# A planned attention kernel: other planned ACT durations in the front, fewer groups in an output phase, output weights split one round after their loads

## The chip, the cores and the metric

The kernel runs on one core of one Trainium2 chip. The time is the device time in microseconds (us) of one execution; the median of three runs is compared. The core has five engines with a queue each: TensorE (PE in the profile, its weight loads PEld), VectorE (DVE), ScalarE (ACT), GpSimd (POOL) and SyncE (SP), which issues transfers. They meet only through semaphores, and each works through its queue in order.

## The reference

A gate mixes two attention branches over the same input x of 2048 positions and 512 features, all in float32.

```python
g = sigmoid((x * gate_w).sum(-1, keepdims=True))
a = A_ref(x, A_wqkv, A_wo)   # 32 heads of 16; each position sees 8 positions, 2 apart, behind it
b = B_ref(x, B_wq, B_wk, B_wv, B_wo)   # 32 query heads of 16, one key and value head, all 2048 positions
return g * a + (1 - g) * b
```

Branch A is a local, dilated attention: softmax over 8 logits for each position and head. Branch B is full attention, where `softmax(q @ k.T / 4)` has 32 x 2048 x 2048 entries. Each branch ends with a product with a 512 x 512 matrix of output weights.

## The kernel before, in words

**Units and steps.** Branch B is cut into 32 units (4 blocks of 512 queries by 8 groups of 4 heads) and each unit into 16 steps of 128 keys. A step computes scores of four heads (two calls of `exp_pair`, L521, each two half matmuls that use 64 rows of the array and run side by side, then one exponential of 1024 columns on ACT, L528) and adds weighted values (`weighted`, L533, eight matmuls of 32 columns at L536) into the bank `po`. There are 512 steps.

**Maxima.** The exponential needs a shift for each query that is near its largest score. So the scores are also computed once ahead of the steps, only for their maxima: 2048 half matmuls in all, of one head pair, 128 queries and 512 keys each. They are made in three forms:
- a *pair* (`fill_pair`, L375): two half matmuls into the bank `pm`, one reduction of 1024 columns on VectorE (L380);
- a *single* (`fill_one`, L384): one half matmul into `ps` or `po`, one reduction of 512 columns (L391);
- a *group* (`fill_diff`, L447, and `fill_sum`, L466): for two blocks of keys, a matmul with half their difference, whose absolute value ACT writes to SBUF (L458), and a matmul with half their sum, which VectorE adds to it and reduces (L471). A group stands for two half maxima. It moves half of the evacuation from VectorE to ACT.

The maxima of a unit must be complete, turned and stored (`filled`, `shift_a` to `shift_d`) before its first step.

**The front.** Before the steps come the projections: keys, then 14 outputs of queries ("q", L1080), then 64 outputs of branch A ("a", four quarters `gg` of 16 blocks of positions, L1081). An output is 12 pairs of half matmuls in one of the banks `pe0` and `pe1`. `stream` (L742) issues them and places singles or groups between them, so that a half of a group runs beside a half of an output. When an output of branch A is done, `a_post` (L244) copies it out with ACT (L258, L259; in the first quarter also L262).

**The planner.** The order of all instructions is fixed while the program is written, by clocks of its own: `clk["pe"]`, `clk["act"]`, `clk["dve"]`, and `pool`. `after(engine, ready, duration)` (L99) moves such a clock. The durations are constants in the code. A group is placed only if `diff_ready` (L440) holds, which among others asks that ACT's clock is at most 0.7 us ahead of TensorE's. If the next maxima are for a group and it isn't ready, the slot passes without a maximum. In the front and in an output phase, slots for groups are the only ones once the keys' sums and differences are formed.

**The steps' maxima.** In each step `fill_ready` (L902) places a pair, and a single if `singles` (L896) says that those that are left need it; a single is not placed in a unit's first step. `pause` (L912) makes maxima between steps when a unit would start without.

**Output phases.** Three times four rows of blocks of output are computed between steps (`out_phase`, L780): for each row transposes, copies and splits on ACT (`prepare` L686, `turn` L695, `out_store` L728), 24 slots of half matmuls, and groups between them through the same `stream`. The last four rows are spread over the last steps (`spread`, L825): the condition for its start stands in the loop of steps (L1184).

**GpSimd's work.** `work` (L992) is a generator of pieces for branch A's local attention on GpSimd, in 16 rounds of two; `run_pool` (L1059) issues pieces as far as 2.5 us ahead of TensorE's clock. From the start of the steps on, a round also takes entries of the list `wos` (L986): `wo_load` (L676) loads 128 rows of output weights through SP into one of two buffers, and `wo_split` (L680) splits them into a high part (ACT, L94) and a rest (GpSimd, L95).

Of the kernel before, what the change touches and what calls it, by code (L numbers as in the profile page):

```python
# [19 lines left out]
C = D // P  # L20
# [4 lines left out]
NU = NQB * NHG  # L25
# [13 lines left out]
NF = 2 * NU * 2 * 4 * 4  # L39
FMAX = 3.4028234e38  # L40
NH = NJ // 2
LEAD, M2S, M1S, PER_ROW = 3.0, 0.5, 0.3, 20


T_R, T_LAT, T_EXP, T_RED2, T_RED1, T_W, T_TTR = 0.23, 0.20, 0.92, 1.14, 0.61, 1.21, 0.66
# [3 lines left out]
def gated_mix_kernel(ctx, tc, xt, wa, wk, wq, wo_a, wo_b, out):  # L49
# [40 lines left out]
    free = {"m2": 0.0, "m1": 0.0, "e0": 0.0, "e1": 0.0, "po": 0.0, "d0": 0.0, "d1": 0.0}  # L90
# [6 lines left out]
    clk = {"pe": 0.0, "act": 0.0, "dve": 0.0}  # L97

    def after(eng, ready, dur):  # L99
        clk[eng] = max(clk[eng], ready) + dur  # L100
        return clk[eng]
# [142 lines left out]
    def a_post(gg, j, x):  # L244

        nonlocal pool
        (bank, key), n = front[x], GN + (0 if gg else VN)
        settle("add", 1)
        if j % 2 == 0:
            settle("store", 1)  # L250
            stage["t"] = p1.tile([P, GC, 2, AN], F32, name="stage", bufs=2)
        st = stage["t"]
        if gg == 0 and j < 3:
            two = wp.tile([P, GN + VN], F32, name="two", tag="aext", bufs=2)
        else:
            two = (p2 if j % 3 else pm)[0].tile([P, GN + VN], F32, name="two", tag=("two", "raw", "own")[j % 3], bufs=1)
        own = st[:, :, j % 2, :]
        nc.scalar.activation(own, bank[:, 0, :GN].rearrange("p (g n) -> p g n", g=GC), AF.Copy)  # L258
        nc.scalar.activation(two[:, :n], bank[:, 1, :n], AF.Copy)  # L259
        if gg == 0:  # L260
            vg = p1.tile([P, VN], F32, name="vg", bufs=2)
            nc.scalar.activation(vg, bank[:, 0, GN:GN + VN], AF.Copy)  # L262
        at = after("act", clk["pe"] + T_LAT, 0.8 if gg else 1.0)
        free[key] = at + 0.1

        def rest():
            nonlocal pool
            nc.gpsimd.tensor_add(own, own, two[:, :GN].rearrange("p (g n) -> p g n", g=GC))
            if gg == 0:
                nc.gpsimd.tensor_add(vst[:, j, 0:DH], vg[:, 0:DH], two[:, GN:GN + DH])  # L270
                nc.gpsimd.tensor_add(gate[:, 1, j:j + 1], vg[:, DH:DH + 1], two[:, GN + DH:GN + DH + 1])
            pool = max(pool, 1e3 * at) + (1000 if gg else 1450)
            if j % 2 == 1:
                dst = ad[gg * GC:(gg + 1) * GC, HALO:, :].rearrange("g (p j) n -> p g (j n)", j=NJ)
                tasks.append((pool / 1e3 + 0.5, lambda: nc.sync.dma_start(dst[:, :, (j - 1) * AN:(j + 1) * AN], st.rearrange("p g j n -> p g (j n)")), (), "store"))
            if j == NJ - 1:
                tasks.append((pool / 1e3 + 1.0, whole, (gg,)))

        tasks.append((at, rest, (), "add"))
# [58 lines left out]
    half = []  # L338
    tasks, shifted, pm = [], set(), []
    hooks, pool, done = [], 0.0, set()  # L340
# [20 lines left out]
    def to_go():  # L361
        return 2 * len(slots) + len(half)
# [33 lines left out]
    sel, dd, pend, group, formed, ended, wants = [], [], [], [], set(), set(), []  # L396
# [43 lines left out]
    def diff_ready():  # L440
        if not group and (ended or half or not hv or not paired()):
            return False
        odd = group[0][4] if group else 0
        now = clk["pe"]
        return len(pend) < len(dd) + 1 and free[f"d{odd}"] <= now + 0.1 and dd[0][1][odd] <= now + 0.9 and clk["act"] <= now + 0.7 and clk["dve"] <= now + 1.8

    def fill_diff():  # L447
        if not group:
            v, pr, t, kc = slots.pop(0)
            slots.pop(0)  # L450
            group.extend([(v, pr, t, kc, 0), (v, pr, t, kc, 1)])
        v, pr, t, kc, odd = group.pop(0)
        dst, until = dd[0]
        if odd:
            dd.append(dd.pop(0))
        half_mm(hv[odd], v, pr, t, kc, 1, odd)
        at = clk["pe"] + T_R + T_LAT
        nc.scalar.activation(dst[:, odd], hv[odd], AF.Abs)  # L458
        at = after("act", max(at, until[odd]), 0.52) + 0.1
        free[f"d{odd}"] = at  # L460
        pend.append((v, pr, t, kc, odd, at, dst, until))

# [56 lines left out]
    pe, pexp, exped = [], {}, {}  # L519
# [22 lines left out]
    obp, shaped = {}, set()  # L542
# [39 lines left out]
    def a_load(g, hf):  # L582
        e = wp.tile([P, HALO + NH, AN], F32, name="aext", bufs=2)
        src = ad[g]
# [3 lines left out]
    def a_scores(g, hf):  # L588
        e = aext[g]
        lg = alog[g] = p2[0].tile([P, W, NH, AG], F32, name="lg", bufs=2)  # L590
        q = e[:, HALO:HALO + NH, 0:AC]
        for w4 in range(0, W, 4):
# [67 lines left out]
    p2b = []  # L660
# [231 lines left out]
    later_rows, spread_at = [], [0.0]  # L892
# [92 lines left out]

    wos = []  # L986
    kcs = [(k, c) for k in range(2) for c in range(C)]
    for i in range(2 * C + 1):
        wos.append([(wo_load, kcs[i])] if i < 2 * C else [])
        wos[-1] += [(wo_split, kcs[i - 1])] if i else []  # L990

    def work():  # L992

        def sub(g, hf):
            yield lambda: ("max", g, hf) in done
            a_sub(g)
            hooks.append((pool + 3000, a_exp, g, ("exp", g, hf)))
            yield 500
            summing.append((g, hf))

        def sums():

            if summing and ("exp",) + summing[0] in done:
                g, hf = summing.pop(0)
                a_add_up(g)
                hooks.append((pool + 800, a_sum, g, ("sum", g, hf)))
                yield 800

        def values(g, hf):
            while ("sum", g, hf) not in done:  # L1010
                if summing:
                    yield lambda: ("exp",) + summing[0] in done
                    yield from sums()
                else:
                    yield lambda: ("sum", g, hf) in done
            yield lambda: g < 8 or p2b
            yield from a_values(g, hf)
            if g == NAG - 1:
                done.add(hf)

        def load(i):
            if i < len(order):
                yield lambda: order[i][0] // GC < ready_gg
                a_load(*order[i])
                yield 600 if i else 6200

        order = [(g, hf) for hf in range(2) for g in range(NAG)]
        extra, summing = list(wos), []
        yield from load(0)
        yield from load(1)  # L1030
        for i in range(0, len(order), 2):
            yield from a_scores(*order[i])
            hooks.append((pool + 3500, a_max, order[i][0], ("max",) + order[i]))
            for k, x in enumerate(a_scores(*order[i + 1])):
                yield x
                if k == 6:
                    yield from sub(*order[i])
                if k == 11:
                    yield from sums()
            hooks.append((pool + 3500, a_max, order[i + 1][0], ("max",) + order[i + 1]))  # L1040
            for k, x in enumerate(values(*order[i])):
                yield x
                if k == 6:
                    yield from sub(*order[i + 1])
                if k == 11:
                    yield from sums()
            yield from load(i + 2)
            yield from values(*order[i + 1])
            yield from load(i + 3)
            for _ in range(2):  # L1050
                if p2b and extra:
                    for f, a in extra.pop(0):
                        f(*a)
                    yield 1300
        assert not extra

    pieces, blocked = [work()], []
# [25 lines left out]
    last = len(lumps) - 1  # L1083
# [76 lines left out]
    for s in range(NS + 1):  # L1160
# [21 lines left out]
        k, n = outs // 4, C - (outs >= NJ - 4)  # L1182
        one = singles(s)
        if outs == NJ - 4:  # L1184
            if NU - 3 in shaped and not half and not one and not later_rows and "last" not in done:
                later_rows.append(spread(list(range(outs, NJ)), n))
            if short > 0 and steps < 2:
                pause(short)
        elif due or outs < NJ and s and kt == 0 and outs // NH in done and NHG * (k + 1) - 1 in shaped and (lead < LEAD or s >= 16 * (NHG * (k + 2) + 1)):
            if not due:  # L1190
                prepare(outs, n)
                due.append(n)
            else:
                out_phase(list(range(outs, outs + 4)), due.pop(), kt == 1)
                outs += 4
                order = (0, "m1", 2)
        elif short > 0 and steps < 2:
            pause(short)
# [83 lines left out]
```

## Time and profile before

| | us |
|---|---|
| median of 3 runs (lowest to highest) | 1512.37 (1512.18 to 1513.42) |
| the profiled execution | 1513.46 |
| its span, first to last instruction | 1511.7 |
| PE, ACT, DVE, POOL busy in it | 1479.3, 1360.6, 1117.5, 1004.4 |

The steps begin at about 319 us; before that is the front. The three output phases stand at about 881 to 917, 1047 to 1084 and 1215 to 1254 us. In the profile a row of a group of instructions names line, engine, operation, the tiles it writes and reads, and how often it stands; behind the bar come busy time, the mean of one in ns, and how long the engine was idle just before them, with what ended that. A busy PE is not a PE at its peak, since matmuls overlap.

### The profile page before, as it was taken

The numbers are of one execution on the slowest core, as the hardware profiler recorded it, in microseconds if no ns is written. First come the engines' busy times: TensorE is split into PE (matmuls) and PEld (weight loads), VectorE is DVE, ScalarE is ACT, GpSimd is POOL, SyncE is SP. The second block draws the span as 40 slices with busy tenths as digits, with TensorE's granted clock in tenths as the row PEclk, the third lists the DMA queues.
The fourth block names the chain that finished last, engine by engine and source line by source line (L and its number), as shares of the span: only waits on it lengthen the run. The fifth ranks groups of instructions, "written<-read, shape, count | busy, mean of one in ns | idle before, by whom it ended". The sixth has DMA issues, their size and how long they took to land.

```text
span 1511.7 us, 29757 instructions
## 1 busy us (share of the span) xinstructions
PE 1479.3 (98%) x10920; PEld 711.6 (47%) x10920; DVE 1117.5 (74%) x1848; ACT 1360.6 (90%) x1802; POOL 1004.4 (66%) x1770
## 2 busy tenths in 40 slices
PE   7999999989999999999999999999999999999998
PEld 4787787843333333333333354334533364333343
DVE  6668788867787787777878877877688887877401
ACT  4789999978999999999999989999899998999975
POOL 6764888877988888888788898888888330000110
PEclk9999999999999999999999999999999999999999
DMA  6542424230212112112112112220211001100000
GB/s 218 148 118 88 136 75 141 67 126 12 94 41 75 59 58 80 41 52 84 52 48 80 41 54 66 69 74 29 91 49 54 13 15 47 33 2 12 12 1 29
DMA packets 48034, 97.60 MB, mean 65 GB/s; under 512 B 10784, under 2 KB 27168, under 8 KB 43792
## 3 DMA queue, kind: packets, MB, share of 16 engines
q1 hardware_dynamic: 41216, 55.99, 12.6%
q0 software_dynamic: 5664, 37.87, 7.5%
q8 instruction: 86, 1.41, 0.4%
q10 hardware_dynamic: 1008, 1.84, 0.3%
q14 instruction: 60, 0.49, 0.1%
HBM read 69.90 MB, written 25.78 MB: 63 GB/s over the span
## 4 chain that ended last, share of the span: by engine, by line
PE 73%; ACT 3%; issue 1%; DVE 1%; DVEq 0%; ACTq 0%; DMA 0%
PE po L536 32%; PE pe L526 23%; PE pm L359 7%; PE pe L792 4%; PE ps L359 3%; ACT pexp L528 2%; PE pd L438 1%; PE ps L438 1%; PE ps L861 1%; PE pm L861 1%; PE po L438 1%; PE pe L699 0%; PE pe L1246 0%; DVE mx L380 0%; ACT woh L94 0%
## 5 line engine op out<-in xcount | busy, mean ns | idle before, releaser
L528 ACT ACTIVATE pexp<-pe 128x1024 f32<-128x1024 f32 x1021 | 982.6, 1023 | 70.1 <-PE pe L526 66.7
L380 DVE TENSOR_REDUCE mx<-pm 128x2 f32<-128x1024 f32 x474 | 579.0, 1221 | 212.2 <-PE pm L359 208.2
L536 PE MATMUL po<-pexp,vst 128*32 128x512 f32 x4096 | 546.8, 606 | 1.2 <-DVE mx L471 0.7
L526 PE MATMUL pe<-qst,kst 64*128 64x512 f32 x2042 | 498.8, 460 | 10.2 <-ACT pexp L528 10.0
L526 PEld LDWEIGHTS pe<-qst,kst 64*128 64x128 f32 x2042 | 197.5, 184 | 509.7 <-ACT pexp L528 497.4
L359 PE MATMUL pm<-kst,qst 62*128 62x512 f32 x951 | 192.2, 399 | 1.9 <-DVE mx L380 1.4
L458 ACT ACTIVATE dd<-pd 128x512 f32<-128x512 f32 x300 | 169.8, 602 | 16.0 <-PE pd L438 4.6
L596 POOL TENSOR_TENSOR pr<-aext 128x256 f32<-128x256 f32 x256 | 182.7, 742 | 0.2
L391 DVE TENSOR_REDUCE mx<-ps 128x1 f32<-128x512 f32 x257 | 174.7, 680 | 4.2 <-PE ps L359 2.1
L656 POOL TENSOR_TENSOR oa<-oa,av 128x256 f32<-128x256 f32 x224 | 164.2, 733 | 15.3
L438 PE MATMUL pd<-kcd,qst 62*128 62x512 f32 x416 | 151.2, 413 | 4.4 <-ACT dd L458 3.9
L536 PEld LDWEIGHTS po<-pexp,vst 128*32 128x32 f32 x4096 | 80.6, 108 | 146.1 <-issue 134.3
L653 POOL TENSOR_TENSOR av<-aext,lg 128x256 f32<-128x256 f32 x224 | 139.7, 624 | 12.1
L1111 PE MATMUL pe<-wah,xl 64*128 64x384 f32 (+1 forms) x504 | 133.9, 348 | 0.0
L1111 PE MATMUL pe<-wah,xh 64*128 64x384 f32 (+1 forms) x504 | 132.3, 345 | 0.3 <-ACT two L220 0.3
L1111 PE MATMUL pe<-wal,xh 64*128 64x384 f32 (+1 forms) x504 | 131.7, 346 | 0.0
L471 DVE CUSTOM_DVE_ANT_0 dd<-ps,dd 128x512 f32<-128x512 f32 x150 | 103.6, 690 | 33.6 <-PE ps L438 13.7
L471 DVE CUSTOM_DVE_ANT_0 dd<-po,dd 128x512 f32<-128x512 f32 x150 | 103.4, 690 | 20.4 <-ACT dd L458 8.0
L359 PE MATMUL ps<-kst,qst 62*128 62x512 f32 x257 | 104.3, 406 | 0.3 <-DVE mx L391 0.3
L562 POOL TENSOR_TENSOR rl<-rl,gate_t 128x16 f32<-128x16 f32 x31 | 6.9, 223 | 143.6 <-DVE rl L556 143.5
L359 PEld LDWEIGHTS pm<-kst,qst 62*128 62x128 f32 x951 | 90.8, 186 | 6.9 <-DVE mx L380 4.0
L438 PE MATMUL ps<-kcd,qst 62*128 62x512 f32 x208 | 89.2, 429 | 1.5 <-DVE mx L471 1.0
(199 smaller groups left out, 2001.1 us busy)
## 6 DMA issues: line engine op xcount, KB each, us to landing
aext<-ad POOLq DMA_DIRECT2D x32, 1056.0 KB, 5.6
qst<-qd SPq DMA_DIRECT2D x122, 128.0 KB
ad<-stage SPq DMA_DIRECT2D x32, 384.0 KB
qst<-qd SPq DMA_DIRECT2D x122, 64.0 KB
xraw<-xt SPq DMA_DIRECT2D x16, 256.0 KB
qd<-qhi SPq DMA_DIRECT2D x16, 256.0 KB
qd<-qlo SPq DMA_DIRECT2D x16, 256.0 KB
out<-two SPq DMA_DIRECT2D x12, 256.0 KB
```

What stands on the lines that cost most here:

```text
L359: nc.tensor.matmul(dst, qst[where[v]][b:b + 62, pr, t * P:(t + 1) * P], kst[b:b + 62, kc * 512:(kc + 1) * 512], start=True, stop=True)
L380: nc.vector.tensor_reduce(m[:, :, pr, t, kc], dst, AX.X, ALU.max)
L391: nc.vector.tensor_reduce(m[:, odd, pr, t, kc:kc + 1], dst, AX.X, ALU.max)
L438: nc.tensor.matmul(dst, qst[where[v]][b:b + 62, pr, t * P:(t + 1) * P], kcd[b:b + 62, kc // 2, x, :], start=True, stop=True)
L458: nc.scalar.activation(dst[:, odd], hv[odd], AF.Abs)
L471: nc.vector.tensor_tensor_reduce(d[:, odd], dst, d[:, odd], 1.0, -FMAX, ALU.add, ALU.max, m[:, odd, pr, t, kc:kc + 1])
L526: nc.tensor.matmul(bank[:, odd, :], kst[b:b + 64, kt * P:(kt + 1) * P], qst[where[u]][b:b + 64, pr, :], start=True, stop=True)
L528: nc.scalar.activation(e, bank, AF.Exp, scale=SCALE)
L536: nc.tensor.matmul(po[32 * i:32 * i + 32, :], vst[:, kt, :], pexp[s, i // 2][:, i % 2, :], start=(kt == 0), stop=(kt == NJ - 1))
L596: nc.gpsimd.tensor_mul(pr[:, k], q, e[:, o:o + NH, AC:2 * AC])
L656: nc.gpsimd.tensor_add(ao, ao, av)
L1111: nc.tensor.matmul(front[2 if x == last else x % 2][0][:, b, :n], l[h], r[h], start=(i == 0), stop=(i == 3 * C - 1))
```

## The change

Four edits, all in the planning code; no instruction gets another shape.

1. The clock of ACT is charged more in the front and for absolute values: an output's copies 1.0 instead of 0.8 us (first quarter 1.25 instead of 1.0), an absolute value 0.55 instead of 0.52 us.
2. `diff_ready` asks that ACT's clock is at most 0.6 instead of 0.7 us ahead (`ACTS`). This and the absolute value's charge hold in the front and in output phases.
3. The list `wos` has 5 entries instead of 9. An entry first splits the two blocks of output weights that the entry before it loaded, and then loads two more. A round takes one entry instead of two, charged 2600 instead of twice 1300 ns.
4. The start of the last rows no longer asks that `singles` says no, but that the maxima left are at most twice the steps up to 14 before unit 31.

```diff
+ACTS = 0.6
...
-        at = after("act", clk["pe"] + T_LAT, 0.8 if gg else 1.0)
+        at = after("act", clk["pe"] + T_LAT, 1.0 if gg else 1.25)
...
-        return ... and clk["act"] <= now + 0.7 and clk["dve"] <= now + 1.8
+        return ... and clk["act"] <= now + ACTS and clk["dve"] <= now + 1.8
...
-        at = after("act", max(at, until[odd]), 0.52) + 0.1
+        at = after("act", max(at, until[odd]), 0.55) + 0.1
...
-    for i in range(2 * C + 1):
-        wos.append([(wo_load, kcs[i])] if i < 2 * C else [])
-        wos[-1] += [(wo_split, kcs[i - 1])] if i else []
+    for i in range(0, 2 * C + 2, 2):
+        wos.append([(wo_split, x) for x in kcs[i - 2:i]] if i else [])
+        wos[-1] += [(wo_load, x) for x in kcs[i:i + 2]]
...
-            for _ in range(2):
-                if p2b and extra:
-                    for f, a in extra.pop(0):
-                        f(*a)
-                    yield 1300
+            if p2b and extra:
+                for f, a in extra.pop(0):
+                    f(*a)
+                yield 2600
...
-            if NU - 3 in shaped and not half and not one and not later_rows and "last" not in done:
+            if NU - 3 in shaped and not half and to_go() <= 2 * max(0, 16 * (NU - 1) - 14 - s) and not later_rows and "last" not in done:
```

More of the change, by code (lines that the diff above doesn't have):

```diff
@@ L444, in diff_ready @@
         now = clk["pe"]
-        return len(pend) < len(dd) + 1 and free[f"d{odd}"] <= now + 0.1 and dd[0][1][odd] <= now + 0.9 and clk["act"] <= now + 0.7 and clk["dve"] <= now + 1.8
+        return len(pend) < len(dd) + 1 and free[f"d{odd}"] <= now + 0.1 and dd[0][1][odd] <= now + 0.9 and clk["act"] <= now + ACTS and clk["dve"] <= now + 1.8
     def fill_diff():
```

## The prediction, made before the result was known

> **What bounds the kernel now.** I read the page's first two parts, then the table of stages, then the groups and waits inside a stage, and last the timeline of single steps. The page's rows are the span with its instructions, and busy time, share of the span and instructions of each engine:
>
> ```profile
> span 1511.7 us, 29757 instructions
> PE 1479.3 (98%) x10920; PEld 711.6 (47%) x10920; DVE 1117.5 (74%) x1848; ACT 1360.6 (90%) x1802; POOL 1004.4 (66%) x1770
> ```
>
> The view of stages gives, for a stretch, its length, then busy time and instructions of PE, PEld, DVE, ACT and POOL, the granted clock, DMA share and GB/s. The stretches are the front's three last quarters of branch A's projections, the stall after it, the exp steps up to the first output phase, that phase, and two stretches of the tail:
>
> ```profile
> 139.00:318.00 179.00, 175.27 (x1611) 143.57 (x1607) 152.09 (x461) 168.22 (x359) 148.65 (x249) 1.00 0.33 103
> 334.00:348.00 14.00, 9.56 (x50) 3.53 (x48) 4.68 (x6) 6.92 (x9) 8.46 (x12) 0.76 0.26 98
> 348.00:880.00 532.00, 530.33 (x3766) 195.29 (x3765) 419.44 (x478) 506.52 (x547) 449.31 (x858) 1.00 0.19 59
> 881.00:917.00 36.00, 35.87 (x310) 25.18 (x310) 30.32 (x85) 30.66 (x56) 33.14 (x56) 1.00 0.10 38
> 1411.00:1429.00 18.00, 16.57 (x111) 5.18 (x107) 5.79 (x9) 17.24 (x21) 3.82 (x7) 1.00 0.09 25
> 1429.00:1489.00 60.00, 59.90 (x348) 25.26 (x350) 0.97 (x2) 46.04 (x55) 7.72 (x8) 1.00 0.00 1
> ```
>
> PE is busy 97% and more nearly everywhere, so busy shares don't tell the bound. In the front two things do: ACT's order of work, and who waits for whom. The timeline of ACT (start, length, instruction, count) shows two outputs of the front, one with four absolute values and one with five; the last rows are waits of the same stretch (total us, times, longest):
>
> ```profile
> 279.75 0.49 ACT L258 ACTIVATE stage<-pe 128x384 f32<-128x384 f32 x1
> 280.60 2.39 ACT L458 ACTIVATE dd<-pd 128x512 f32<-128x512 f32 x4
> 282.88 0.48 ACT L258 ACTIVATE stage<-pe 128x384 f32<-128x384 f32 x1
> 283.69 2.98 ACT L458 ACTIVATE dd<-pd 128x512 f32<-128x512 f32 x5
> 286.58 0.48 ACT L258 ACTIVATE stage<-pe 128x384 f32<-128x384 f32 x1
> PEld pd L438 <- ACT dd L458: 15.0, 50, 0.8
> PEld ps L438 <- DVE mx L471: 9.1, 28, 1.3
> ```
>
> An output with four groups takes 3.13 us (279.75 to 282.88), with five 3.70 us (282.88 to 286.58). The difference, 0.57 us, is one absolute value. ACT runs without a gap there, and TensorE waits for it 50 times. So ACT is the bound of the front, and a group costs its ACT time.
>
> In the exp steps ACT (506.52 of 532 us, 95%) and TensorE are both near their limit. Three steps, by TensorE's timeline:
>
> ```profile
> 370.69 1.07 PE L536 MATMUL po<-pexp,vst 128*32 128x512 f32 x8
> 372.59 1.07 PE L536 MATMUL po<-pexp,vst 128*32 128x512 f32 x8
> 374.15 0.39 PE L359 MATMUL ps<-kst,qst 62*128 62x512 f32 x1
> 374.71 1.06 PE L536 MATMUL po<-pexp,vst 128*32 128x512 f32 x8
> ```
>
> The step from 370.69 lasts 1.90 us. The next, with one more single maximum (ps), lasts 2.12 us. A single added to a step costs 0.22 us.
>
> **The change part by part.**
>
> *Front: fewer groups.* The planner puts a group (one absolute value on ACT, two half matmuls, one reduction on VectorE) where its ACT clock allows it. An output of branch A has 24 half matmuls; the plan takes 0.18 us for a pair of them and 0.23 us for a slot with a half of a group, so its length is 2.16 + 0.28 g for g groups. ACT is charged 0.8 + 0.52 g + r, where r is what else is charged and left idle. I take r from the groups that there are:
>
> ```profile
> L458 ACT ACTIVATE dd<-pd 128x512 f32<-128x512 f32 x300 | 169.8, 602 | 16.0 <-PE pd L438 4.6 <-DVE mx L471 2.3 <-PE po L438 1.1
> L458 ACT ACTIVATE dd<-pd 128x512 f32<-128x512 f32 x214 | 120.9, 600 | 8.7 <-PE pd L438 3.6 <-PE pe L1111 0.2
> L458 ACT ACTIVATE dd<-pd 128x512 f32<-128x512 f32 x58 | 33.0, 608 | 2.9 <-PE pd L438 0.7 <-PE pe L1111 0.5 <-DVE mx L471 0.5
> ```
>
> These are the groups of the whole front (27 to 319 us), of the 48 outputs with 384 columns (139 to 318), and of the first quarter (87 to 139, 14 of its 16 outputs). Of the 48: 214/48 = 4.46 groups, length 3.41, so r = 3.41 - 0.8 - 2.32 = 0.29. With the new charges, 1.0 + 0.55 g + 0.29 = 2.16 + 0.28 g gives g = 3.2, so 1.24 fewer, 59 in all. First quarter: 58/14 = 4.14, r = 3.32 - 1.0 - 2.15 = 0.17; with 1.25 and 0.55, g = 2.7, so 1.4 fewer, 22 in 16 outputs. The query outputs, whose copies keep their charge, lose about 4 in all by 0.03 us a group and the tighter gate. Together some 85 of 300 go (bounds 40, if the gate matters less than this balance says, and 100).
>
> What a group gives back in the front lies between 0.57 us (ACT alone) and the TensorE time of its two half matmuls, 2 x 175.27/1611 = 0.22 us. I take 0.52, near the upper end, because at 3.2 groups ACT still needs about 3.13 - 0.8 x 0.57 = 2.7 us and the other charges of such an output, while TensorE comes close behind. 85 x 0.52 = **44 us less**. The stage adds of GpSimd (148.65 of 179 us busy) are the next late work; branch A's pieces there simply move behind the front.
>
> *Exp steps: the maxima come back.* A group covers two half maxima. They return as singles in the exp steps, because the pairs already run once a step:
>
> ```profile
> L380 DVE TENSOR_REDUCE mx<-pm 128x2 f32<-128x1024 f32 x468 | 571.6, 1221 | 207.1 <-PE pm L359 203.1
> L391 DVE TENSOR_REDUCE mx<-ps 128x1 f32<-128x512 f32 x249 | 169.2, 679 | 2.7 <-PE ps L359 2.1 <-PE pe L792 0.6
> 1117.38:1150.71 33.33, 7.44 (x11) 1.00 0.26 87
> 491.79:524.28 32.49, 5.44 (x8) 1.00 0.17 55
> ```
>
> There are 249 singles after the front. The last two rows are stretches of 16 steps with 11 and 8 singles (VectorE's busy time in L391): (33.33 - 32.49)/3 = 0.28 us each, against 0.22 by the step above. I take 0.24. 170 from the front and 20 from the output phases (below) cost 190 x 0.24 = **46 us more**.
>
> *Output phases: the absolute value's charge and the gate.* A row has 24 slots of 0.23 us, so 5.52 + 0.23 g against ACT's 2.4 + 0.52 g + r. The groups by shape count 116 absolute values in 12 rows, 9.67 a row:
>
> ```profile
> L458 ACT ACTIVATE pexp<-pd 128x512 f32<-128x512 f32 x116 | 65.9, 598 | 11.7 <-PE pd L438 5.4 <-issue 1.3 <-PE pe L792 0.7
> ```
>
> So r = 7.74 - 7.43 = 0.31, and with 0.55 g becomes 8.8: 10 groups fewer, 20 singles more. ACT is busy 30.66 of 36 us there, so a group gives back between 0.57 and 0.22 us; 10 x 0.45 = **4.5 us less**.
>
> *Output weights.* Today the first round issues two loads, splits the first at once, and ACT, whose queue runs in order, stands until that load lands. The second round is the second group of rows:
>
> ```profile
> 333.85 1.03 SPq L678 DMA_DIRECT2D os<-wo_a  x2
> 334.62 1.06 PE L536 MATMUL po<-pexp,vst 128*32 128x512 f32 x8
> 338.53 0.63 ACT L94 ACTIVATE woh<-os 128x512 fp32r<-128x512 f32 x1 [4.46 <-issue]
> 340.12 0.79 PE L526 MATMUL pe<-qst,kst 64*128 64x512 f32 x2 [4.44 <-ACT pexp L528]
> 342.12 1.93 PE L536 MATMUL po<-pexp,vst 128*32 128x512 f32 x8
> 348.12 1.07 PE L536 MATMUL po<-pexp,vst 128*32 128x512 f32 x8
> ...
> 402.35 1.15 ACT L94 ACTIVATE woh<-os 128x512 fp32r<-128x512 f32 x2
> 402.94 1.06 PE L536 MATMUL po<-pexp,vst 128*32 128x512 f32 x8
> 403.07 2.51 POOL L95 TENSOR_TENSOR wol<-os,woh 128x512 fp32r<-128x512 f32 x2 [0.28 <-ACT woh L94]
> 405.82 1.07 PE L536 MATMUL po<-pexp,vst 128*32 128x512 f32 x8
> ```
>
> Three steps take 334.62 to 348.12, 13.50 us, where two of 2.12 and one of 1.90 would take 6.14: 7.4 us lost. TensorE stands 4.44 us, and then runs at half clock for a while: 0.76 over 14 us is 14 x 0.24/0.5 = 6.7 us at half speed (a weighted sum takes 1.93 instead of 1.07 us). The change removes this: no split stands in the first round. In later rounds both splits read data loaded a round, some 60 us, before, and cost as now: the step from 402.94 takes 2.88 us instead of 2.12. The last round has two splits instead of one, 0.75 us. Net **6.6 us less**. The Trainium skill ("TensorE: Matmul & The Clock Gate", the section on HAM oscillation) says that a gap over about 3.4 us throttles the clock, at a price of throttled time times the missing share. By it the stall would be an estimated 4.4 + 6.7 x 0.5 = 7.8 us; the trace agrees with 7.4.
>
> The new loads stand behind their round's splits, since they reuse the buffers: on SP they wait for GpSimd's 2.51 us, and loads of queries and of shifts queue behind them. That I cost at nothing: these are issued for units that lie several units of 16 steps ahead. If that lead were under one unit, each round would cost up to 2.5 us.
>
> *Start of the last rows.* The condition is asked from unit 30 on, where its right side is zero, so it means "no maxima left", as the old one in effect does. TensorE still has ACT-bound steps behind the last maxima (17.24 of 18 us ACT, 1411 to 1429). Nothing, while the maxima end before unit 31.
>
> The sum: -44 + 46 - 4.5 - 6.6 = -9 us. The profiled execution took 1513.46 us (span 1511.7), so 1504.4; the median of the runs is 1.1 us lower: **1503 us**.
>
> **The rivals.**
>
> *TensorE bounds the front already (slower).* Its 175.27 of 179 us busy speak for it. Then a group gives back only 0.22 us: 85 x 0.22 = 19 instead of 44, so 1503 + 25 = 1528. It decides below 0.4 us a group. Against it: 0.57 us between the outputs of four and five groups, and the 50 waits for ACT. The Trainium skill ("Perfetto Trace Analysis", Identifying the Most-Contended Engine) calls matmul busy time no measure of this, and the busy share of weight loads the better one; by it, with 143.57 of 179 us, a fifth of the front is free.
>
> *The singles find no place (slower).* 249 + 190 = 439 singles have 30 units x 15 steps = 450 places. Over that, or where VectorE (1.22 + 0.68 us in a step of 2.12) comes late, maxima are made in pauses, at the 1.22 us of a pair's reduction. 40 that find no place cost 40 x (0.61 - 0.24) = 15 us: 1518. It decides at about 200 singles more than now.
>
> *The plan hardly changes.* Some 15 to 40 groups go. Each trades 0.52 us for 0.48, so only the weights and the output phases count: 1513.5 - 1.1 - 7 = 1505.
>
> *Singles are nearly free.* If ACT, busy 95%, were the bound of a step, a single would hide to a good part, say at 0.14 us: 27 instead of 46 us, 1484. The steps of 2.12 and 1.90 speak against it.
>
> **How the numbers follow.** Chances: my sum (1496 to 1510) 0.53, plan hardly changed 0.12, singles nearly free 0.12, no place 0.15, TensorE-bound front 0.08. A measurement of this kernel tells about 0.2%, 3 us, from no change. Faster by more: 0.72; within: 0.09; slower: 0.19. The range 1486 to 1518 leaves out half of the free singles and the TensorE-bound front; the likeliest case alone has 1496 to 1510.
>
> **What would show it.** Front: about 215 absolute values instead of 300, first exp step near 275 us instead of 319, ACT still above 90% busy. Exp steps: about 440 singles, stretches of 16 steps at some 34 us. Output phases: about 106 absolute values. Weights: no gap of ACT before the first split, no half clock but at the ends. The prediction is wrong if the first exp step comes later than 290 us, if stretches take over 35 us, or if a new gap stands where loads wait for splits.

## The result, and the profile after

The changed kernel takes 1513.12 us (median of 12 runs, 1512.63 to 1515.01) against 1512.61 us (12 runs) of the kernel before: ratio 1.0004, 95% interval 0.9995 to 1.0013. No change can be measured, where 1503 us and a gain of 9 us were forecast. The profiled execution took 1513.99 us. All parts of the change did take place, and they cancel.

The page of the changed kernel, its span and busy times:

```profile
span 1511.9 us, 29552 instructions
PE 1485.9 (98%) x10920; PEld 703.3 (47%) x10920; DVE 1150.4 (76%) x1847; ACT 1329.6 (88%) x1732; POOL 1003.4 (66%) x1774
```

ACT has 31 us less to do and VectorE 33 us more: maxima moved from groups to singles. The source lines of the changed kernel stand one number higher (L459 for L458, and so on). First the groups of ACT in the front (27 to 294.5 us), then VectorE's after the front, then the absolute values of the output phases:

```profile
L459 ACT ACTIVATE dd<-pd 128x512 f32<-128x512 f32 x238 | 133.5, 597 | 20.7 <-PE pd L439 12.8 <-DVE mx L472 1.3 <-PE pe L1111 1.0
L381 DVE TENSOR_REDUCE mx<-pm 128x2 f32<-128x1024 f32 x469 | 572.5, 1221 | 155.2 <-PE pm L360 150.8
L392 DVE TENSOR_REDUCE mx<-ps 128x1 f32<-128x512 f32 x376 | 255.3, 679 | 1.2 <-PE ps L360 1.2
L459 ACT ACTIVATE pexp<-pd 128x512 f32<-128x512 f32 x112 | 63.6, 598 | 16.7 <-PE pd L439 12.7 <-PE pe L793 0.3 <-ACT turned L707 0.3
```

238 absolute values stand in the front instead of 300 (62 fewer; 85 were forecast), 112 instead of 116 in the output phases (4 fewer; 10 forecast), and 376 singles in the steps instead of 249 (one of the 249 stands just before the first step).

Where the time went, by the starts of each step's first weighted sum (L536, L537) in the two traces:

| us | before | after |
|---|---|---|
| first step begins | 319.6 | 294.7 |
| steps 0 to 479, without the three with an output phase | 984.8 | 1009.6 |
| the three steps with an output phase | 113.9 | 114.2 |
| from step 480 to the end of the last instruction that is counted as busy | 90.0 | 89.8 |

The span itself ends some 3.5 us later in both. The front is 24.9 us shorter. The steps take back the same 24.8 us, although the stall of 334 us is gone. The stretches that answer to those of before: the last three quarters of the front, the steps up to the first output phase, and two stretches of the tail:

```profile
140.00:294.00 154.00, 152.29 (x1465) 131.34 (x1462) 116.66 (x352) 139.02 (x297) 132.82 (x218) 1.00 0.36 115
296.00:797.00 501.00, 499.25 (x3501) 180.50 (x3501) 418.15 (x497) 465.29 (x502) 428.26 (x816) 1.00 0.19 62
1411.00:1429.00 18.00, 17.08 (x118) 5.87 (x114) 9.97 (x15) 17.07 (x20) 3.51 (x6) 1.00 0.00 1
1429.00:1489.00 60.00, 59.73 (x348) 25.09 (x350) 0.97 (x2) 46.20 (x55) 7.97 (x9) 1.00 0.03 8
```

In the front ACT is now busy 139.02 of 154 us, 90% instead of 94%. Its timeline shows two outputs with four groups each, and below it stand the waits of that stretch (140 to 290 us):

```profile
229.77 0.49 ACT L259 ACTIVATE stage<-pe 128x384 f32<-128x384 f32 x1
230.97 2.27 ACT L459 ACTIVATE dd<-pd 128x512 f32<-128x512 f32 x4 [0.33 <-PE pd L439]
233.18 0.49 ACT L259 ACTIVATE stage<-pe 128x384 f32<-128x384 f32 x1
234.43 2.27 ACT L459 ACTIVATE dd<-pd 128x512 f32<-128x512 f32 x4 [0.38 <-PE pd L439]
236.68 0.49 ACT L259 ACTIVATE stage<-pe 128x384 f32<-128x384 f32 x1
PEld pd L439 <- ACT dd L459: 8.5, 33, 0.6
ACT dd L459 <- PE pd L439: 8.3, 30, 0.6
```

These two outputs take 3.41 and 3.50 us, and ACT stands in each until TensorE delivers. TensorE waits for ACT (8.5 us) about as long as ACT for TensorE (8.3 us). In the steps, stretches of 16 with 11 and 14 singles (VectorE's busy time in L392):

```profile
463.77:497.13 33.36, 7.47 (x11) 1.00 0.14 46
1073.96:1107.93 33.97, 9.51 (x14) 1.00 0.14 44
1350.31:1384.36 34.05, 9.51 (x14) 1.00 0.05 14
```

The output weights' rows of the changed kernel (least, median and longest duration in ns, first and last start): the loads begin at 306.3 us and the first split at 382.5 us, and no ACT instruction waits for a load any more.

```profile
L95 ACT ACTIVATE woh<-os x8: 629/631/635, 382.5 to 566.5; 128x512 fp32r<-128x512 f32 x8
L679 SPq DMA_DIRECT2D os<-wo_a x4: 357/370/414, 306.3 to 385.8; - x4
L679 SPq DMA_DIRECT2D os<-wo_b x4: 352/356/360, 445.7 to 508.1; - x4
```

### The profile page after: what moved, and what is told of

Same layout as the page of the kernel before. It is cut to its first block, busy times and chain, and to the rows that moved or that the text cites. A ratio compares the mean times of both kernels' runs of the same rounds, so it can differ in the third digit from the quotient of the medians.

```text
span 1511.9 us, 29552 instructions
## 1 busy us (share of the span) xinstructions
PE 1485.9 (98%) x10920; PEld 703.3 (47%) x10920; DVE 1150.4 (76%) x1847; ACT 1329.6 (88%) x1732; POOL 1003.4 (66%) x1774
## 4 chain that ended last, share of the span: by engine, by line
PE 91%; ACT 4%; DVE 2%; issue 1%; DMA 1%; POOL 1%; SPq 0%; DVEq 0%; ACTq 0%; POOLq 0%
PE po L537 32%; PE pe L527 24%; PE pe L1111 9%; PE pm L360 7%; PE ps L360 4%; PE pe L793 4%; PE pd L439 3%; PE ps L439 2%; ACT pexp L529 2%; PE po L439 2%; PE ps L862 1%; PE pm L862 1%; PE pe L194 1%; DMA xraw<-xt 1%; ACT dd L459 0%
## 5 line engine op out<-in xcount | busy, mean ns | idle before, releaser
L537 PE MATMUL po<-pexp,vst 128*32 128x512 f32 x4096 | 545.5, 605 | 1.2 <-DVE mx L472 0.7
L527 PE MATMUL pe<-qst,kst 64*128 64x512 f32 x2042 | 540.8, 457 | 4.6 <-ACT pexp L529 4.5
L527 PEld LDWEIGHTS pe<-qst,kst 64*128 64x128 f32 x2042 | 219.8, 184 | 465.3 <-ACT pexp L529 452.2
L392 DVE TENSOR_REDUCE mx<-ps 128x1 f32<-128x512 f32 x385 | 261.5, 679 | 2.7 <-PE pe L1111 1.5
L360 PE MATMUL ps<-kst,qst 62*128 62x512 f32 x385 | 162.3, 422 | 0.4 <-DVE mx L392 0.3
L537 PEld LDWEIGHTS po<-pexp,vst 128*32 128x32 f32 x4096 | 80.6, 108 | 168.2 <-issue 156.9
L459 ACT ACTIVATE dd<-pd 128x512 f32<-128x512 f32 x238 | 133.5, 597 | 20.7 <-PE pd L439 12.8
L654 POOL TENSOR_TENSOR av<-aext,lg 128x256 f32<-128x256 f32 x224 | 139.3, 622 | 12.9
L1111 PE MATMUL pe<-wah,xh 64*128 64x384 f32 (+1 forms) x504 | 124.5, 341 | 0.5 <-ACT vg L263 0.4
L439 PE MATMUL pd<-kcd,qst 62*128 62x512 f32 x350 | 121.0, 408 | 2.5 <-ACT dd L459 2.2
L472 DVE CUSTOM_DVE_ANT_0 dd<-ps,dd 128x512 f32<-128x512 f32 x119 | 82.1, 690 | 48.8 <-PE ps L439 23.0
L472 DVE CUSTOM_DVE_ANT_0 dd<-po,dd 128x512 f32<-128x512 f32 x119 | 82.0, 689 | 23.3 <-PE po L439 14.7
L360 PEld LDWEIGHTS ps<-kst,qst 62*128 62x128 f32 x385 | 70.9, 184 | 60.5 <-DVE mx L392 56.0
```

The costliest lines, as they stand in the source:

```text
L360: nc.tensor.matmul(dst, qst[where[v]][b:b + 62, pr, t * P:(t + 1) * P], kst[b:b + 62, kc * 512:(kc + 1) * 512], start=True, stop=True)
L392: nc.vector.tensor_reduce(m[:, odd, pr, t, kc:kc + 1], dst, AX.X, ALU.max)
L439: nc.tensor.matmul(dst, qst[where[v]][b:b + 62, pr, t * P:(t + 1) * P], kcd[b:b + 62, kc // 2, x, :], start=True, stop=True)
L472: nc.vector.tensor_tensor_reduce(d[:, odd], dst, d[:, odd], 1.0, -FMAX, ALU.add, ALU.max, m[:, odd, pr, t, kc:kc + 1])
L527: nc.tensor.matmul(bank[:, odd, :], kst[b:b + 64, kt * P:(kt + 1) * P], qst[where[u]][b:b + 64, pr, :], start=True, stop=True)
L537: nc.tensor.matmul(po[32 * i:32 * i + 32, :], vst[:, kt, :], pexp[s, i // 2][:, i % 2, :], start=(kt == 0), stop=(kt == NJ - 1))
```

## Experiments: the parts apart

Theory 1: the edit of the weights is worth what was forecast, and moving groups out of the front costs as much. Theory 2: the stall's time is lost again behind it, and the move is neutral. Four kernels tell them apart.

**Only the weights' edit.** The kernel before with part 3 of the change:

```diff
-    for i in range(2 * C + 1):
+    for i in range(0, 2 * C + 2, 2):
...
-                    yield 1300
+                yield 2600
```

> Only the output weights' edit on the kernel before; charges, gate and the start of the last rows as before. Theory 1 (the stall is worth what its steps lost, and moving groups costs as much as the edit of the weights gives): three steps no longer take 7.4 us too long, no split waits for a load, no half clock after 319 us, and the time is 7 us under the kernel before, ratio 0.995 to 0.996. Theory 2 (what the stall cost is lost again somewhere behind it, the move of groups is neutral): ratio 0.999 to 1.001.

Measured: 1506.78 us (5 runs), ratio 0.9961 (0.9948 to 0.9973). The place of the stall, 334 to 348 us, in this kernel:

```profile
334.00:348.00 14.00, 14.00 (x105) 5.24 (x101) 10.21 (x11) 13.20 (x15) 13.16 (x26) 1.00 0.28 106
```

TensorE runs 105 matmuls there instead of 50, at full clock. The ordinary steps take 978.2 us instead of 984.8: 6.6 us, the forecast term. Theory 2 falls.

**All but the weights' edit.** The changed kernel with the list of before:

```diff
-    for i in range(0, 2 * C + 2, 2):
+    for i in range(2 * C + 1):
...
-                yield 2600
+                    yield 1300
```

> The changed kernel with the output weights' list of the kernel before. Theory 1: the front ends some 25 us earlier as in the changed kernel, the exp steps give back 32 us, and the stall of 7 us is there: 7 us over the kernel before, ratio 1.004 to 1.006. Theory 2: ratio 0.999 to 1.001.

Measured: 1518.79 us (5 runs), ratio 1.0041 (1.0029 to 1.0054). So the other three parts together cost about 6 us. The stall is there too, in a later round: the ordinary steps take 1015.1 us, 5.5 more than in the changed kernel. Here the trace names the load as its cause:

```profile
  ACT woh L95: 8.1, 6
  DMA os<-wo_b: 5.0, 1
```

These are the waits of the instructions that touch the loaded weights (us, times): one split waits 5.0 us for its load.

**Charges or gate.** The changed kernel with the gate of before, and the changed kernel with the charges of before:

```diff
-ACTS = 0.6
+ACTS = 0.7
```

> The changed kernel with ACT's gate at 0.7 us again, so weights and charges are changed and the gate is not. If the charges move the groups (theory 1): 240 absolute values in the front, give or take 8, and a time within 3 us of the changed kernel. If it is the gate: 285 or more, and the time of the weights' edit alone.

```diff
-        at = after("act", clk["pe"] + T_LAT, 1.0 if gg else 1.25)
+        at = after("act", clk["pe"] + T_LAT, 0.8 if gg else 1.0)
...
-        at = after("act", max(at, until[odd]), 0.55) + 0.1
+        at = after("act", max(at, until[odd]), 0.52) + 0.1
```

> The changed kernel with the planned durations of before, so weights and gate are changed and the charges are not. Theory 1: 290 absolute values in the front, give or take 8, and a time within 3 us of the weights' edit alone, some 5 to 8 us under the kernel before. If the gate is what loses: the changed kernel's time.

Measured: charges without the gate 1514.28 us (11 runs), ratio 1.0012 (1.0002 to 1.0021), 242 groups in the front. Gate without the charges 1504.80 us (5 runs), ratio 0.9948 (0.9935 to 0.9960), 292 groups. The charges move the groups and lose the time; the kernel with the gate has 8 groups fewer than the weights' edit alone and is 2 us faster. It also has part 4 of the change, the start of the last rows, which was not tested apart. This kernel, "weights and gate" from here on, is the fastest version of this study and beats both kernels; these are its page's span and its row of the front's absolute values:

```profile
span 1502.6 us, 29737 instructions
L459 ACT ACTIVATE dd<-pd 128x512 f32<-128x512 f32 x292 | 164.5, 600 | 16.8 <-PE pd L439 6.0 <-DVE mx L472 2.0 <-PE pe L1111 1.4
```

## Experiments: what bounds the front

The prediction took ACT as the front's bound. Eight kernels add work to one engine for each of the 64 outputs of branch A, which the planner doesn't know of, so that the order of all else stays. Each ran once, so only lengths inside the trace are read, from the first to the last copy of an output. The added instructions, at the end of the copies or at an output's first pair:

```diff
+        probe = wp.tile([P, 64], F32, name="probe", bufs=2)
+        nc.scalar.activation(probe, ident[:, 0:64], AF.Copy)
...
+        probe = wp.tile([P, 256], F32, name="probe", bufs=1)
+        nc.scalar.activation(probe, kst[:, 0:256].bitcast(F32), AF.Abs)
...
+        probe = wp.tile([P, 1], F32, name="probe", bufs=1)
+        nc.vector.tensor_reduce(probe, kst[:, 0:512].bitcast(F32), AX.X, ALU.max)
...
+        if lump[0] == "a" and i == 0:
+            nc.tensor.matmul(front[...][0][:, b, :n], l[h], r[h], start=True, stop=True)
```

A small copy on ACT, before and after:

> The kernel before with one more small ACT copy (64 columns) for each output of branch A in the front, which the plan does not know of; the order of everything else is unchanged. Its own length is some 0.2 us. If ACT bounds the front of before: 64 times 0.2, the first exp step 10 to 14 us later. If TensorE does: under 4 us.

> The changed kernel with the same extra ACT copy. If its front is now bound by TensorE: the first exp step under 5 us later. If ACT still bounds it: 10 to 14 us later.

The doubled first pair on TensorE:

> The kernel before, each output of branch A issues its first pair of half matmuls twice (the second overwrites the first), unknown to the plan: 64 times 0.18 us of TensorE. If ACT bounds the front of before: the first exp step under 5 us later. If TensorE does: 10 to 12 us later.

> The changed kernel with the same doubled first pair of half matmuls. If TensorE bounds its front now: the first exp step 8 to 12 us later. If ACT still does: under 4 us later.

A larger instruction on ACT:

> The kernel before with a larger extra ACT instruction (256 columns, about 0.39 us) for each output of branch A, unknown to the plan: 64 x 0.39 = 25 us of ACT. The first added copy of 0.27 us made the front 4.6 us longer of 17, a doubled pair of matmuls 5.2 of 11.5. If ACT and TensorE bound the front of before by turns, the 256 columns show with 8 to 14 us; if ACT alone does, with 20 to 25.

> The changed kernel with the same extra ACT instruction of about 0.39 us. By turns, with TensorE ahead now: 3 to 8 us. If ACT alone bounds: 20 to 25.

A reduction on VectorE:

> The kernel before with one extra reduction of 512 columns on VectorE for each output of branch A (about 0.6 us, 64 x 0.6 = 38 us of VectorE). If VectorE's part of a group counts in the front: over 10 us later first step. If it is covered: under 5 us.

> The changed kernel with the same extra reduction on VectorE. With fewer groups VectorE has more room: under 5 us if the front is bound by TensorE and ACT only; over 10 us if by VectorE.

First the copies without an addition, in the kernel before and in the changed one. The first start of the first row and the last start of the second bound the length (91.3 to 318.8 us, and 91.3 to 293.8):

```profile
L258 ACT ACTIVATE stage<-pe x63: 474/487/548, 91.3 to 314.8; 128x384 f32<-128x384 f32 x63
L258 ACT ACTIVATE stage<-pm x1: 492/492/492, 318.8 to 318.8; 128x384 f32<-128x384 f32 x1
L259 ACT ACTIVATE stage<-pe x63: 462/487/529, 91.3 to 290.3; 128x384 f32<-128x384 f32 x63
L259 ACT ACTIVATE stage<-pm x1: 490/490/490, 293.8 to 293.8; 128x384 f32<-128x384 f32 x1
```

The rows of the larger ACT instruction in the kernel before: its own durations, and the first and the last copy:

```profile
L264 ACT ACTIVATE probe<-kst x64: 417/429/497, 92.4 to 332.5; 128x256 f32<-128x256 f32 x64
L258 ACT ACTIVATE stage<-pe x63: 472/487/542, 91.5 to 327.6; 128x384 f32<-128x384 f32 x63
L258 ACT ACTIVATE stage<-pm x1: 490/490/490, 331.7 to 331.7; 128x384 f32<-128x384 f32 x1
```

The same in the changed kernel, and then the doubled pair in the changed kernel:

```profile
L259 ACT ACTIVATE stage<-pe x63: 463/488/520, 90.5 to 294.0; 128x384 f32<-128x384 f32 x63
L259 ACT ACTIVATE stage<-pm x1: 492/492/492, 297.5 to 297.5; 128x384 f32<-128x384 f32 x1
```

```profile
L259 ACT ACTIVATE stage<-pe x63: 460/488/527, 90.6 to 296.1; 128x384 f32<-128x384 f32 x63
L259 ACT ACTIVATE stage<-pm x1: 491/491/491, 299.5 to 299.5; 128x384 f32<-128x384 f32 x1
```

Without an addition the length is 227.5 us before and 202.5 us after. The kernels with only the weights' edit, and with all but it, have the same two fronts, and the same two lengths to 0.1 us; so differences of a few us can be read from single runs. What each addition made of it (the copy's and the reduction's times are medians of their rows; the pair's 0.18 us is the planner's):

| added for each output | in all | longer before | longer after |
|---|---|---|---|
| ACT, 0.27 us | 17 us | 4.7 | 1.6 |
| ACT, 0.43 us | 27 us | 12.7 | 4.5 |
| VectorE, 0.68 us | 44 us | 8.1 | 1.7 |
| TensorE, 0.18 us | 12 us | 5.3 | 6.4 |

The expectations were about the start of the first step, which came later by 5.1 and 1.1 us (small copy, before and after), 5.6 and 5.8 (pair), 12.9 and 3.7 (larger instruction), 8.0 and 0.7 (reduction). Four missed: small copy, pair and reduction in the kernel before, and the pair in the changed kernel, all came out between the two answers that they offered. The larger instruction was forecast from the first four results, with both engines bounding the front by turns, and came true.

If ACT alone had bounded the front of before, 0.27 us more of ACT would have shown nearly in full. It showed by a quarter, and TensorE's addition by 5.3 of 12 us. So before, both count, and neither alone is the bound. ACT's part fits with its idle time: it was idle for 10.8 of the 179 us of the last three quarters, 0.22 us for each output. An addition of that size finds room; of the next 0.16 us (10 us in all, from the small to the larger instruction) 8.0 us show. After, an addition to ACT shows by a sixth or less, one to TensorE by half: TensorE counts most. It isn't the only bound there either, since the other half of its addition doesn't show; what hides it was not tested. VectorE counted a little before (8.1 of 44 us) and hardly does now.

## Experiments: are the prices constant?

Two kernels between 292 and 238 groups, both with the weights' edit and the gate:

```diff
+        at = after("act", clk["pe"] + T_LAT, 0.85 if gg else 1.05)
...
+        at = after("act", max(at, until[odd]), 0.53) + 0.1
```

> Weights and gate as changed, and the planned ACT durations only a quarter to a third of the way: copies 0.85 (first quarter 1.05), absolute value 0.53. The plan has 284 groups in the front instead of 292. If the price curve bends (a group gives 0.5 us while ACT still binds, and a single costs 0.1 us while the steps are bound by ACT): within 2 us of weights and gate, 1503 to 1506 us. If prices are constant at 0.40 a group and 0.25 a single: 8 x 0.1 = 1 us slower than weights and gate, 1505.5.

```diff
+        at = after("act", clk["pe"] + T_LAT, 0.9 if gg else 1.1)
```

> Weights and gate as changed, copies half the way (0.9, first quarter 1.1), absolute value at 0.52. The plan has 272 groups in the front, and some 305 singles in the steps. If the curve bends: 37 more singles at up to 0.28 us against 20 groups at 0.4, 1505 to 1508 us. If prices are constant: 20 x 0.1 and the output phases' part, 1507 to 1508.

Measured: 1507.57 us (5 runs, 1505.72 to 1507.76), ratio 0.9965 (0.9953 to 0.9978), and 1509.74 us (11 runs), ratio 0.9979 (0.9970 to 0.9988). The first missed both expectations by about 2 us, the second both by about as much; it also has 326 singles where 305 were expected. These two ran on another chip than the four kernels of the parts, and the kernel before took 1512.3 us there against 1513.1 us. The kernels that have the weights' edit, in a row; lengths are those of the profiled execution, by the same starts of steps as above, and the time is the median (the profiled execution of the kernel with 272 groups was 1.5 us faster than its median):

| groups in the front | singles in the steps | first step | ordinary steps 0 to 479 | time |
|---|---|---|---|---|
| 300 (weights alone) | 248 | 319.9 | 978.2 | 1506.8 |
| 292 (weights and gate) | 268 | 316.0 | 979.8 | 1504.8 |
| 284 | 281 | 314.5 | 983.8 | 1507.6 |
| 272 | 326 | 306.3 | 994.7 | 1509.7 |
| 242 (no gate) | 377 | 297.3 | 1010.3 | 1514.3 |
| 238 (the change) | 376 | 294.7 | 1009.6 | 1513.1 |

From 300 to 238 a group gives back 25.1/62 = 0.40 us, and from 248 to 376 a single costs 31.4/128 = 0.245 us. The first 20 singles cost 0.08 us each, later ones 0.24 to 0.31. That would fit a price that is low while the steps still have room, but it rests on one difference of about 3 us, and the five runs of the kernel with 284 groups alone differ by 2; so a bend isn't shown. For the group's price the points scatter too much (0.2 to 0.7 us between neighbours) to say anything of the kind. What is shown are the two averages.

## Why the prediction was wrong

It was wrong above all in one term, the 44 us of the front. The step that failed is the reading "ACT is the bound of the front, and a group costs its ACT time", with 0.57 us for it and 0.52 taken. By the prediction's own sign it was wrong too: the first step comes at 294.7 us, later than 290.

- *The price of a group in the front: 0.52 us taken, 0.40 measured.* The prediction read two outputs of 3.13 and 3.70 us in which "ACT runs without a gap". But a row of the timeline joins instructions of a kind over short gaps. Here are the absolute values of these two outputs, with an idle time of 0.2 us before them, and the second and the third of the first output one by one (start, length):

```profile
L458 ACT ACTIVATE dd<-pd 128x512 f32<-128x512 f32 x9 | 5.2, 598 | 0.2
281.09 0.60 ACT L458 ACTIVATE dd<-pd 128x512 f32<-128x512 f32 x1
281.78 0.60 ACT L458 ACTIVATE dd<-pd 128x512 f32<-128x512 f32 x1
```

In the trace the four absolute values of the first output start at 280.60, 281.09, 281.78 and 282.38 us. Where work waits for ACT, the next one starts 0.50 us later, before the one ahead has ended. The third starts 0.09 us after the end of the second, and the fourth at the end of the third: both came when TensorE had delivered. So the 0.57 us were no price of ACT alone but already a mixture. In the whole stretch of 179 us ACT was idle 8.7 us before its absolute values, 8.3 of them waiting for TensorE; before 83 of the 214 it was idle, mostly for under 0.15 us. TensorE's 50 waits for ACT came to 15.0 us, 8% of the stretch. The two outputs were also a small sample: in the last three quarters of the kernel before, the 20 outputs with four groups take 3.46 us in the mean (3.13 to 3.86), the 23 with five 3.91, which is 0.45 us apart. In the changed kernel 18 outputs with three groups take 3.05 us and 21 with four 3.49. The added work shows the same: both engines count, and neither alone. 62 groups x 0.12 us are 7.4 us, most of the miss of 9.5 us; nearly all of the rest is in the output phases.

- *The number of groups: 85 taken, 62 measured.* The balance of the planner's two clocks gave 3.2 groups for an output of the last three quarters, the trace has 161/48 = 3.35; in the first quarter 2.7 against 49/16 = 3.06. The old mean was also a little high: counted by quarters it is 206/48 = 4.29, since the stretch from 139 us begins inside the first quarter. This hardly matters for the time, since a group that stays costs on one side what it saves on the other: with 62 groups and the forecast's own prices the sum is still -9 us (62 x 0.52 = 32 less, 132 singles x 0.24 = 32 more, 2 and 6.6 less).
- *The price of a single: 0.24 us taken, 0.245 measured.* Right.
- *Output phases: 4.5 us less taken, 0.3 us more measured.* 4 groups went instead of 10, and no gain shows: the three steps took 113.4 to 114.3 us in all kernels with 112 or 116 groups and no added work. In the changed kernel ACT is idle 16.7 us before its absolute values there, 12.7 of them waiting for TensorE, against 11.7 and 5.4 before. Whether the price of 0.45 us was wrong too stays open: in the two kernels with 108 groups, 8 fewer than before, these steps took 110.9 us (charges without the gate) and 112.2 us (copies half the way), which is 0.2 to 0.4 us a group.
- *Output weights: 6.6 us less taken, 6.6 us measured.* Right in mechanism and size: the first split's wait for its load, TensorE's standstill, the half clock behind it (granted clock 0.50 from 341 to 346 us). The Trainium skill ("TensorE: Matmul & The Clock Gate", the section on HAM oscillation) says that a gap of over about 3.4 us throttles; the trace agrees: with the gap of 4.44 us gone, the clock stays full there.
- *SP's queue and the start of the last rows: nothing taken, nothing measured.* The weights' edit alone gave its full 6.6 us in the steps, so loads that queue on SP took nothing from it that shows. The tail is 89.8 us against 90.0.

Of the rivals, the one that came nearest is "TensorE bounds the front already": its point of decision, 0.4 us a group, is where the price lies. Its time of 1528 us didn't come, as TensorE was one bound of two. "The singles find no place" didn't come true; 376 found theirs. The busy share of weight loads, which the Trainium skill ("Perfetto Trace Analysis", Identifying the Most-Contended Engine) sets above matmul busy time, spoke for a fifth of free TensorE; it is 131.34 of 154 us in the changed front, 85%, and TensorE counts there by half of what is added to it. In this case that share didn't show how much TensorE counts.

## What to carry to other kernels

A price that is read from two neighbouring stretches is one sample, and a timeline that joins instructions hides short waits. Take the price from long stretches, look at the idle time beside the busy time, or add known work to one engine and see how much of it shows. Where work is moved between two stages that are both full, the gain is the difference of two prices. Here an error in one of them, 0.52 for 0.40 us, was nearly as large as the whole forecast gain; so test such a move apart from an edit that removes a stall. When an engine's queue runs in order, a load that it needs belongs a round earlier than its use: here that alone was worth 6 us.

## What the runs showed of the hardware that was not expected

An instruction's duration isn't what it takes from a full queue. On ACT a copy of 384 columns lasts 0.49 us and an absolute value of 512 columns 0.60 us, but where work waits the next instruction starts 0.37 us after a copy (279.75 to 280.12) and 0.50 us after an absolute value (280.60 to 281.09). The planner's 0.8 us for two copies and 0.52 us for an absolute value were close to that; the 1.0 and 0.55 us of the change lie nearer to the durations, and with them ACT waits more for TensorE in the front (busy 90% instead of 94%) and the kernel loses the time that the weights' edit gives. And a stall of under 5 us at one load cost 6.6 us in all, since TensorE worked at half clock for some 6.7 us after it.
